# Chunked retention followed by a top-2 mixture of adapters: how the last, half-length chunk is routed, added up and stored

## The chip, the cores and the metric

The kernel runs on one core of a Trainium2 chip. The metric is the device time in microseconds (us) of one execution; the time before is 184.84 us, the median of three runs (184.58 to 186.25).

## What is computed

The reference has two parts. The first is retention: causal attention without a softmax, in which the score of query token i and key token j of a head is weighted with a power of that head's decay. There are 8 batches, 8 heads, 576 tokens and a head size of 64. The second is a mixture of eight low-rank adapters that works on each of the 4608 token rows of 512 numbers, with two experts per token, and adds its result to the row.

```python
# retention, per batch and head
scores = (q @ k.T) / sqrt(64)
D[i, j] = gamma[h] ** (i - j) if i >= j else 0.0
x = (scores * D) @ v                      # heads side by side: x is 4608 x 512
# mixture of adapters, per token row of x
logits = x @ w_gate                       # 8 experts
w = softmax of the two largest logits
delta = sum over those two experts e of  w[e] * ((x @ A[e]) @ B[e])   # A[e]: 512x16, B[e]: 16x512
out = x + delta
```

## The kernel before

**Tiling.** The 576 tokens of a batch are cut into four chunks of 128 tokens and one last chunk of 64. A unit of work in a full chunk is two batches, and each batch is one token tile g of 128 rows. In the last chunk a unit is four batches, because 64 tokens of two batches are put on the 128 partitions of one tile: rows 0 to 63 belong to one batch and rows 64 to 127 to the next. There are 18 units. The last chunk is units 16 and 17, called h and n in the code (lines 748 to 786), and each of them has two token tiles, g = 0 and g = 1.

**Stages.** Helpers named by a letter put one stage of a unit into the queues.

- stage_S, stage_Q and stage_R compute the retention output xT of a unit, with the feature on the partitions.
- stage_B(t) transposes xT back with TensorE and so starts the sum for the output in PSUM: tile po, one bank for each half cc of the head pairs, and in each bank the two token tiles g = 0, 1 side by side.
- stage_Z(t, gs) multiplies xT by the router and by all A at once into the PSUM tile pz; VectorE then takes the largest logits (MAX8, tile m) and the bias ns.
- stage_V computes the two routing weights with a sigmoid on ScalarE (tile sg). stage_W makes the mask cm and the weighted low-rank values zc on VectorE. It calls stage_V itself if that has not been done.
- stage_X transposes zc with TensorE (pzt) and ScalarE copies the result to zT.
- stage_Y multiplies zT by B, adding to po, copies po to the SBUF tile osb and stores osb to memory.

**Order.** Each engine works through its own queue in the order of the program: mm, vec and act (lines 80 to 87) chain every instruction to the one before it on its engine, and the profile shows their line numbers (81 for TensorE, 84 for VectorE, 87 for ScalarE). The order of the stages at the end is written out by hand in lines 748 to 786. PSUM has eight banks, which `bank` and `done` (lines 102 to 110) hand out in a ring, so that the bank that has been free longest is used next.

**The end of the kernel.** The routing of unit n is put in between: the product for g = 0 (stage_Z and stage_V), then stage_Y of unit h, then the product for g = 1, and stage_W for both afterwards. Then follow stage_B(n), two stage_X and two stage_Y. With `spread=True` stage_Y lets VectorE copy the half cc = 1 and ScalarE the half cc = 0.

**The stores.** In a full chunk each token tile is one transfer of 128 rows of 2 KB (line 606). In the last chunk each token tile is two transfers of 64 rows, one for each batch (line 611). They are put into the queue of SyncE, except that in the last unit the second of the two goes into the queue of ScalarE:

```python
            for x in range(2):
                n0 = S * (HALF * g + 2 * qd + x) + C * c
                q_ = nc.scalar if last and x == 1 else nc.sync
                q_.dma_start(out=out[n0 : n0 + L, :], in_=of[rows(x), g, :])
```

Of the kernel before, what the change touches and what calls it, by code (L numbers as in the profile page):

```python
# [18 lines left out]
def kernel(  # L19
# [63 lines left out]
    def vec(fn, **kw):  # L83
        chain("dve", getattr(nc.vector, fn)(**kw))  # L84

    def act(fn, **kw):
        chain("act", getattr(nc.scalar, fn)(**kw))  # L87
# [14 lines left out]
    def bank(shape, name, dtype=FP32):  # L102

        n = free.pop(0)
        x = pp.tile(shape, dtype, tag=f"bank{n}", name=name)
        held[id(x)] = n, x
        return x

    def done(*tiles):
        free.extend(held.pop(id(x))[0] for x in tiles)  # L110
# [141 lines left out]
    def rows(g):  # L252
        return slice(64 * g, 64 * g + 64)
# [215 lines left out]
            s["xT"].append(xt)  # L469
        done(*px)  # L470

    def stage_B(t):

        s = st[t]
        po = [bank([128, 2, HP, Dh], f"po{cc}") for cc in range(2)]
        for g in range(2):
            for dt in range(HP):
                for cc in range(2):
                    mm(
                        po[cc][:, g, dt, :],  # L480
                        lhsT=s["xT"][g][rows(cc), dt, :],
                        rhs=id64[rows(cc), :],
                        is_transpose=True,
                        start=(g == 0 and dt == 0),
                        stop=False,
                        skip_group_check=True,
                    )
        s["po"] = po

    BOTH = (0, 1)  # L490

    def stage_X(ts, gs=BOTH):
        todo = [(t, g) for t in ts for g in gs]
        n = len(todo)
        pzt = bank([128, n, 128], "pzt", FP16)
        for y, (t, g) in enumerate(todo):
            mm(
                pzt[:, y, :], lhsT=st[t]["zc"][g], rhs=ident16,
                is_transpose=True, start=True, stop=True,
            )  # L500
        zt = mo.tile([128, n, 128], FP16, tag=f"zT{n}", name="zT", bufs=2)
        act("copy", out=zt, in_=pzt)
        done(pzt)
        for y, (t, g) in enumerate(todo):
            st[t].setdefault("zT", {})[g] = zt[:, y, :]
# [32 lines left out]
    def stage_V(t, gs=BOTH):  # L538
        s = st[t]
        n = len(gs)  # L540
        lg, m8, ns, pz = s[("route", gs)]
        sg = mo.tile([128, n, E], FP32, tag=f"sg{n}", name="sg")
        for y in range(n):
            act(
                "activation",
                out=sg[:, y, :], in_=lg[:, y, :], func=AFT.Sigmoid,
                bias=ns[:, y : y + 1], scale=2.0,
            )
        s[("route", gs)] += (sg,)
# [23 lines left out]
            s.setdefault("zc", {})[g] = zc[:, y, :]  # L573
        done(pz)

    def stage_Y(t, gs=BOTH, spread=False, last=False):
        c, qd, sl = units[t]
        s = st[t]
        po = s["po"]
        if gs[0] == 0:  # L580
            s["osb"] = outp.tile([128, 2, HP, 2, Dh], FP32, tag="osb", name="osb")
        osb = s["osb"]
        bv = Bcat.rearrange("p (a o d) -> p a o d", a=HP, o=2)
        for cc in range(2):
            for g in gs:
                mm(
                    po[cc][:, g, :, :],
                    lhsT=s["zT"][g],
                    rhs=bv[:, :, cc ^ g, :],
                    start=False,  # L590
                    stop=True,
                    skip_group_check=True,
                )
        for cc in range(2):
            for g in gs:
                if spread and cc == 1:
                    vec("tensor_copy", out=osb[:, g, :, cc ^ g, :], in_=po[cc][:, g])
                else:
                    act("copy", out=osb[:, g, :, cc ^ g, :], in_=po[cc][:, g])
        if gs[-1] == 1:  # L600
            done(*po)
        of = osb.rearrange("p g a o d -> p g (a o d)")
        for g in gs:
            if c < NFULL:
                n0 = S * (QUAD * qd + 2 * sl + g) + C * c
                nc.sync.dma_start(out=out[n0 : n0 + C, :], in_=of[:, g, :])
                continue
            for x in range(2):
                n0 = S * (HALF * g + 2 * qd + x) + C * c
                q_ = nc.scalar if last and x == 1 else nc.sync  # L610
                q_.dma_start(out=out[n0 : n0 + L, :], in_=of[rows(x), g, :])  # L611

    issue(0)
    issue(1)
# [37 lines left out]
    for t in range(NU):  # L652
        if units[t][2] == 0:
            issue(quads.index(units[t][:2]) + 2, (0, 1, 2) if t <= LATE else (0,))
        if t == 0:
            spin(10)
            first_T()
            scale_k(0)
            fill_pick(3)
            gp.dma_start(  # L660
                out=AW[0][:, :, ER : ER + E], in_=moe_w_gate.rearrange("(t p) e -> p t e", p=128)
            )
            for ho in range(2):
                act("copy", out=asc[1][rows(ho)], in_=asc[0][rows(1 - ho)])
            act(
                "copy", out=gdec.rearrange("p a b d -> p a (b d)"),
                in_=gde.unsqueeze(2).broadcast_to((128, HP, 2 * Dh)),
            )
            stage_S(0)
            stage_U(0)  # L670
            stage_Q(0)
            stage_R(0)
            place_A()
            for ho in range(2):
                gp.tensor_copy(out=AW[1][rows(ho)], in_=AW[0][rows(1 - ho)])
            gp.dma_start(out=Bcat, in_=moe_B.rearrange("e r d -> (e r) d"))
            stage_T(1, ("qT",))
            stage_T(1, ("kT",), shared=True)
            scale_k(1)
            stage_Z(0)  # L680
            stage_S(1)
            stage_W(0)
            stage_U(1)
            stage_Q(1)
            stage_R(1)
            stage_T(2, ("qT",))
            stage_B(0)
            stage_X([0])
            stage_Z(1)
            stage_V(1)  # L690
            stage_Y(0, spread=True)
            stage_T(2, ("kT",), shared=True)
            stage_T(3)
            scale_k(2)
            scale_k(3)
            stage_S(2)
            stage_W(1)
            stage_S(3)
            for u in (2, 3):
                stage_U(u)  # L700
                stage_Q(u)
                stage_R(u)
            late_T(4)
            for ho in range(2):
                gp.tensor_tensor(
                    out=maskh[ho], in0=trih.unsqueeze(1).broadcast_to((128, HP, L)),
                    in1=heads(1, ho, L), op=ALU.mult,
                )
            continue
        if t < 4 or units[t][2] or not is_full(t):  # L710
            continue

        before, near = [u for u in (t - 4, t - 3) if u > 0], (t - 2, t - 1)
        here = (t, t + 1)
        for u in here:
            for b, nm in enumerate(("qT", "kT")):
                stage_S(u, (b,))
                if t > LATE:
                    stage_T(u + 2, (nm,))
            if t > LATE:  # L720
                scale_k(u + 2)
        for u in before:
            stage_B(u)
        stage_X(before)
        stage_Z(near[0])
        stage_V(near[0])
        for u in before:
            stage_Y(u)
        stage_Z(near[1])
        stage_V(near[1])  # L730
        if t > LATE:
            issue(t // 2 + 2, (1,))
        if units[t][0] > 0:
            for u in here:
                stage_Q(u)
        for u in near:
            stage_W(u)
        for u in here:
            if t > LATE and u == here[1]:
                issue(t // 2 + 2, (2,))  # L740
            stage_U(u)
            if units[t][0] == 0:
                stage_Q(u)
            stage_R(u)
        if t <= LATE:
            late_T(t + 2)
# [6 lines left out]
    stage_X([h - 4, h - 3])  # L753
    stage_Z(h - 2)
    stage_V(h - 2)
    stage_Y(h - 4, spread=True)
    stage_Y(h - 3, spread=True)
    stage_W(h - 2)
    stage_R(h)
    stage_S(n)  # L760
# [10 lines left out]
    stage_W(h)  # L771
    stage_R(n)
    stage_B(h)
    stage_Y(h - 1, spread=True)
    stage_X([h])
    stage_Z(n, (0,))
    stage_V(n, (0,))
    stage_Y(h, spread=True)
    stage_Z(n, (1,))
    for g in range(2):  # L780
        stage_W(n, (g,))
    stage_B(n)
    for g in range(2):
        stage_X([n], (g,))
    for g in range(2):
        stage_Y(n, (g,), spread=True, last=True)
# [1 line left out]
_INS = ['q', 'k', 'v', 'moe_w_gate', 'moe_A', 'moe_B']  # L788
_OUTS = [((4608, 512), 'float32')]
# [25 lines left out]
```

## Time and profile before

| | before |
|---|---|
| time, median of three runs | 184.84 us |
| span of the profiled execution | 183.6 us |
| TensorE busy | 174.5 us (95%) |
| VectorE busy | 115.4 us (63%) |
| ScalarE busy | 66.8 us (36%) |
| GpSimd busy | 58.2 us (32%) |
| memory traffic | 209 GB/s over the span |
| last computing instruction | starts at 179.27 us, takes 0.37 us |
| last two stores issued | 179.67 us |

The span is the time from the first to the last event of the profiled execution. The share of busy time tells which engine carries the kernel as a whole; the change is in the last 10 us, and there it is the order of waits that counts. In a timeline line the first number is the start in us from the beginning of the span, the second the duration in us; then follow engine, line, operation, output and inputs, and in square brackets how long the engine stood idle before it, and what it was waiting for. SPq and ACTq are the queues of SyncE and ScalarE, in which the transfers are issued.

### The profile page before, as it was taken

How to read it: one execution, taken by the hardware profiler on the slowest of the kernel's cores; microseconds unless marked ns; L12 is line 12 of the kernel's file. 1: busy time of each engine (PE TensorE's matmuls, PEld its weight loads, DVE VectorE, ACT ScalarE, POOL GpSimd, SP SyncE). 2: the span in 40 equal slices, each digit the busy share in tenths (PEclk: the TensorE clock that was granted, in tenths of full speed). 3: DMA queues.
4: the chain of work that ended last, by engine and by line, in shares of the span. 5: the costliest groups of instructions: out<-in, count | busy, mean ns of one | idle time of the engine just before them, and what ended most of it. 6: DMA issues, size and time to landing. Idle time of an engine off the chain costs nothing. (4 is left out here: it accounts for less than half of the span.)

```text
span 183.6 us, 8103 instructions
## 1 busy us (share of the span) xinstructions
PE 174.5 (95%) x3606; PEld 163.2 (89%) x3606; DVE 115.4 (63%) x294; ACT 66.8 (36%) x179; POOL 58.2 (32%) x69
## 2 busy tenths in 40 slices
PE   7898999999999999999999999999999999999970
PEld 2698989989999999989999999999999999999850
DVE  3785956969566926764468626781679248385660
ACT  3602054061406150475602751175307550132540
POOL 8877016062029202676023802262040005000000
PEclk9999999999999999999999999999999999999997
DMA  6999979899898998897699899997880060033175
GB/s 143 277 257 253 282 223 263 248 279 260 224 272 235 248 323 231 241 290 240 175 335 288 238 280 283 287 222 137 287 177 4 0 225 10 4 115 122 74 245 144
DMA packets 53283, 38.74 MB, mean 211 GB/s; under 512 B 26992, under 2 KB 48640, under 8 KB 53248
## 3 DMA queue, kind: packets, MB, share of 16 engines
q1 hardware_dynamic: 50688, 37.23, 71.8%
q10 hardware_dynamic: 2384, 0.85, 1.8%
q8 instruction: 28, 0.46, 1.0%
q0 software_dynamic: 176, 0.15, 0.5%
q14 instruction: 7, 0.06, 0.1%
HBM read 28.91 MB, written 9.44 MB: 209 GB/s over the span
## 5 line engine op out<-in xcount | busy, mean ns | idle before, releaser
L84 DVE TENSOR_TENSOR rt<-ps,mask 128x512 f32<-128x512 f32 x64 | 40.4, 684 | 9.6 <-PE ps L81 9.0
L264 POOL TENSOR_TENSOR k<-k,pack 128x512 f32<-128x512 f32 x32 | 32.6, 1044 | 26.9 <-PE pkT L81 19.5
L81 PE MATMUL pz<-AW,xT 128*128 128x136 f32 x288 | 37.2, 282 | 0.0
L423 POOL TENSOR_TENSOR P<-pn,gdec 128x512 f32<-128x512 f32 x12 | 15.3, 1278 | 68.2 <-DVE pn L84 64.0
L81 PE MATMUL ps<-qT,kT 64*128 64x128 f32 x512 | 34.8, 279 | 0.3 <-issue 0.3
L81 PEld LDWEIGHTS pz<-AW,xT 128*128 128x128 f32 x288 | 34.7, 190 | 0.2
L81 PEld LDWEIGHTS ps<-qT,kT 64*128 64x128 f32 x512 | 31.3, 188 | 1.7 <-issue 1.0
L81 PE MATMUL px<-rt,v 128*64 128x128 f32 x512 | 30.7, 273 | 0.0
L87 ACT COPY qT<-pqT 128x512 f32<-128x512 f32 (+1 forms) x33 | 16.8, 568 | 31.2 <-PE pqT L81 31.1
L81 PEld LDWEIGHTS px<-rt,v 128*64 128x64 f32 x512 | 27.7, 137 | 0.0
L84 DVE TENSOR_TENSOR xT<-px,asc 128x512 f32<-128x512 f32 x36 | 24.4, 688 | 4.0 <-PE px L81 2.6
L87 ACT COPY kT<-pkT 128x512 f32<-128x512 f32 x29 | 16.0, 600 | 27.7 <-PE pkT L81 17.8
L84 DVE COPY lg<-pz 128x16 f32<-128x16 f32 x17 | 3.0, 174 | 32.6 <-PE pz L81 32.6
L81 PE MATMUL pu<-v,k 128*64 128x64 f32 x512 | 18.1, 224 | 0.0
L87 ACT COPY osb<-po 128x256 f32<-128x256 f32 x60 | 17.5, 387 | 1.4 <-PE po L81 0.8
L81 PEld LDWEIGHTS pu<-v,k 128*64 128x64 f32 x512 | 16.6, 138 | 1.4 <-issue 1.0
L87 ACT ACTIVATE sg<-lg,ns 128x8 f32<-128x8 f32 x34 | 8.4, 293 | 25.2 <-DVE ns L84 24.8
L81 PE MATMUL pkT<-id,k 64*128 64x64 f32 x288 | 13.1, 225 | 1.5 <-DMA k<-in_k_dram 1.4
L81 PE MATMUL px<-qT,P 64*64 64x128 f32 (+1 forms) x512 | 14.3, 259 | 0.0
L81 PEld LDWEIGHTS pkT<-id,k 64*128 64x128 f32 x288 | 11.4, 139 | 2.8 <-issue 0.9
L84 DVE TENSOR_TENSOR pn<-pu,P 128x512 f32<-128x512 f32 x12 | 8.3, 692 | 8.3 <-PE pu L81 8.3
L81 PEld LDWEIGHTS px<-qT,P 64*64 64x64 f32 x512 | 12.6, 133 | 0.9
(54 smaller groups left out, 149.4 us busy)
## 6 DMA issues: line engine op xcount, KB each, us to landing
out_dram<-osb SPq DMA_DIRECT2D x32, 256.0 KB, 3.5
v<-in_v_dram SPq DMA_DIRECT2D x4, 512.0 KB, 7.1
q<-in_q_dram SPq DMA_DIRECT2D x3, 512.0 KB, 5.3
k<-in_k_dram SPq DMA_DIRECT2D x3, 512.0 KB, 7.3
out_dram<-osb SPq DMA_DIRECT2D x6, 128.0 KB, 2.3
q<-in_q_dram SPq DMA_DIRECT2D x2, 256.0 KB, 4.1
k<-in_k_dram ACTq DMA_DIRECT2D x2, 256.0 KB, 4.7
Arow<-in_moe_A_dram SPq DMA_DIRECT2D x1, 256.0 KB, 6.6
```

The costliest lines, as they stand in the source:

```text
L81: chain("pe", nc.tensor.matmul(*args, **kw))
L84: chain("dve", getattr(nc.vector, fn)(**kw))
L87: chain("act", getattr(nc.scalar, fn)(**kw))
L264: gp.tensor_tensor(out=kk[:, b], in0=kk[:, b], in1=gv[:, 0].unsqueeze(2).broadcast_to((128, H, Dh)), op=ALU.mult,)
L423: nc.gpsimd.tensor_tensor(out=Pt, in0=pn, in1=gdec, op=ALU.mult)
```

## The change

Three things are changed, all of them for the last chunk.

1. The stores of a token tile of the last chunk become one transfer from all 128 partitions. The destination is addressed as two batches of 64 rows of 512 numbers. All of them are issued from SyncE.
2. The two products for the routing of unit n stand one after the other, each followed at once by its sigmoid and its weighting, and stage_Y of unit h comes after both. The first transpose of stage_X(n) comes before stage_B(n), the second after it.
3. With `split=True` stage_B gives each token tile g of unit n PSUM banks of its own (pn, four banks), so that the matmuls for g = 1 don't share a bank with copies that read g = 0.

The aim is shorter waits at the end of the kernel and fewer, fuller transfers. `spread=True` becomes `copies=("act", "dve")`, which makes the same copies on the same engines; the third choice, a copy by GpSimd, is not used by any call. The core of the diff:

```diff
-    def stage_B(t):
+    def stage_B(t, split=False):
         s = st[t]
-        po = [bank([128, 2, HP, Dh], f"po{cc}") for cc in range(2)]
+        if split:
+            s["banks"] = {(cc, g): bank([128, HP, Dh], f"pn{cc}") for g in range(2) for cc in range(2)}
+            s["po"] = s["banks"]
+        else:
+            s["banks"] = {cc: bank([128, 2, HP, Dh], f"po{cc}") for cc in range(2)}
+            s["po"] = {(cc, g): s["banks"][cc][:, g] for g in range(2) for cc in range(2)}
+        po = s["po"]
...
-                        po[cc][:, g, dt, :],
+                        po[(cc, g)][:, dt, :],
...
-                        start=(g == 0 and dt == 0),
+                        start=((split or g == 0) and dt == 0),
...
         for g in gs:
             if c < NFULL:
                 n0 = S * (QUAD * qd + 2 * sl + g) + C * c
                 nc.sync.dma_start(out=out[n0 : n0 + C, :], in_=of[:, g, :])
                 continue
-            for x in range(2):
-                n0 = S * (HALF * g + 2 * qd + x) + C * c
-                q_ = nc.scalar if last and x == 1 else nc.sync
-                q_.dma_start(out=out[n0 : n0 + L, :], in_=of[rows(x), g, :])
+            b0 = HALF * g + 2 * qd
+            nc.sync.dma_start(
+                out=out.rearrange("(b s) d -> b s d", s=S)[b0 : b0 + 2, C * c : C * c + L, :],
+                in_=of[:, g, :],
+            )
...
-    stage_Y(h - 1, spread=True)
+    stage_Y(h - 1, copies=("act", "dve"))
     stage_X([h])
-    stage_Z(n, (0,))
-    stage_V(n, (0,))
-    stage_Y(h, spread=True)
-    stage_Z(n, (1,))
     for g in range(2):
+        stage_Z(n, (g,))
+        stage_V(n, (g,))
         stage_W(n, (g,))
-    stage_B(n)
+    stage_Y(h, copies=("act", "dve"))
+    stage_X([n], (0,))
+    stage_B(n, split=True)
+    stage_X([n], (1,))
     for g in range(2):
-        stage_X([n], (g,))
-    for g in range(2):
-        stage_Y(n, (g,), spread=True, last=True)
+        stage_Y(n, (g,), copies=("act", "dve"))
```

More of the change, by code (lines that the diff above doesn't have):

```diff
@@ L487, in stage_B @@
                     )
-        s["po"] = po
     BOTH = (0, 1)
@@ L574, in stage_W, with stage_Y @@
         done(pz)
-    def stage_Y(t, gs=BOTH, spread=False, last=False):
+    def stage_Y(t, gs=BOTH, copies=("act", "act")):
         c, qd, sl = units[t]
@@ L586, in stage_Y @@
                 mm(
-                    po[cc][:, g, :, :],
+                    po[(cc, g)],
                     lhsT=s["zT"][g],
@@ L595, in stage_Y @@
             for g in gs:
-                if spread and cc == 1:
-                    vec("tensor_copy", out=osb[:, g, :, cc ^ g, :], in_=po[cc][:, g])
+                o, i = osb[:, g, :, cc ^ g, :], po[(cc, g)]
+                if copies[cc] == "act":
+                    act("copy", out=o, in_=i)
+                elif copies[cc] == "dve":
+                    vec("tensor_copy", out=o, in_=i)
                 else:
-                    act("copy", out=osb[:, g, :, cc ^ g, :], in_=po[cc][:, g])
+                    chain("pool", gp.tensor_copy(out=o, in_=i))
         if gs[-1] == 1:
-            done(*po)
+            done(*s["banks"].values())
         of = osb.rearrange("p g a o d -> p g (a o d)")
@@ L690 @@
             stage_V(1)
-            stage_Y(0, spread=True)
+            stage_Y(0, copies=("act", "dve"))
             stage_T(2, ("kT",), shared=True)
@@ L755 @@
     stage_V(h - 2)
-    stage_Y(h - 4, spread=True)
-    stage_Y(h - 3, spread=True)
+    stage_Y(h - 4, copies=("act", "dve"))
+    stage_Y(h - 3, copies=("act", "dve"))
     stage_W(h - 2)
```

## The prediction

> **What bounds the kernel now.** I read the row of busy shares first (TensorE 95% over the span), then the slices: in the last two TensorE reads 7 and 0 and the transfers 7 and 5, so the tail is another stage with other limits, and the change touches it alone. The chain of waits, followed back from the last instruction, ends like this (start, duration, what):
>
> ```profile
> 178.18 0.43 DVE osb L84
> 178.61 0.02 issue
> 178.63 0.02 ACTq L611
> 178.65 0.04 issue
> 178.69 0.54 ACTq L611
> 179.23 0.04 issue
> 179.27 0.37 ACT osb L87
> ```
>
> ScalarE's last copy waits behind its own 0.54 us of issuing a store. The timeline of the tail shows a second wait there:
>
> ```profile
> 175.34 0.76 DVE L84 COPY osb<-po 128x256 f32<-128x256 f32 x2
> 176.27 0.17 DVE L84 MAX8 m<-pz 128x8 f32<-128x8 f32 x1 [0.17 <-PE pz L81]
> 177.30 0.29 DVE L84 TENSOR_TENSOR zc<-pz,cm 128x128 f16<-128x128 f32 x1
> 178.11 0.37 ACT L87 COPY osb<-po 128x256 f32<-128x256 f32 x1
> 178.53 0.39 PE L81 MATMUL po<-Bcat,zT 128*128 128x256 f16 x2 [0.40 <-ACT osb L87]
> 179.27 0.37 ACT L87 COPY osb<-po 128x256 f32<-128x256 f32 x1 [0.78 <-PE po L81]
> 179.67 0.50 ACTq L611 DMA_DIRECT2D out_dram<-osb  x1
> ```
>
> The matmuls for g = 1 wait 0.40 us until the copies of g = 0 have left the shared bank. Arithmetic ends at 179.64 us and the last two stores are issued at 179.67. By the answers on single issues these land 2.5 us (SyncE) and 2.8 us (ScalarE) later, at 182.5, and the span ends 1.1 us after that, at 183.6. So the tail is: last copy, issue, landing, 1.1 us of closing. The time outside the profile is 184.84 - 183.6 = 1.24 us more.
>
> The stores themselves (DMA groups of the page; KB each, us from issue to landing):
>
> ```profile
> out_dram<-osb SPq DMA_DIRECT2D x32, 256.0 KB, 3.5
> out_dram<-osb SPq DMA_DIRECT2D x6, 128.0 KB, 2.3
> out_dram<-osb ACTq DMA_DIRECT2D x2, 128.0 KB, 2.7
> ```
>
> And the rate while stores stream (windows; the last two columns are the share of the 16 DMA engines and GB/s):
>
> ```profile
> 174.40:174.80 0.40, 0.40 (x6) 0.40 (x5) 0.17 (x1) 0.16 (x1) 0.00 (x0) 1.00 1.05 410
> 175.60:176.00 0.40, 0.40 (x6) 0.40 (x4) 0.40 (x2) 0.40 (x3) 0.00 (x0) 1.00 1.06 405
> 178.40:178.80 0.40, 0.27 (x2) 0.10 (x1) 0.20 (x1) 0.09 (x1) 0.00 (x0) 1.00 0.99 231
> 179.20:179.60 0.40, 0.00 (x0) 0.00 (x0) 0.18 (x1) 0.33 (x1) 0.00 (x0) 1.00 1.02 220
> ```
>
> With all 16 engines busy, stores of 128 rows move 405 to 410 GB/s (first two lines), stores of 64 rows 220 to 231 (last two). That speaks for full-height stores. It also gives the price used below: 408/16 = 25.5 GB/s for one engine, so **one row of 2048 bytes costs one engine 80 ns**; with the share of 1.05 divided out it is 84 ns. I take 82.
>
> **What the Trainium skill says.**
> 1. "DMA: Bandwidth & Descriptors", section "Why a DMA increments its semaphore by 16 and not by 1", tells how many of the 16 engines a transfer runs on: the slowest dimension of size above 1 is taken of each of the two access patterns, and the number is the largest one up to 16 that divides both; from SyncE and ScalarE the lowest-numbered engines are used. The trace agrees where it can: every transfer in it has 64 or 128 as its slowest dimension, and stores fill all 16 engines. It holds no transfer with a small outer dimension.
> 2. The same page, "Rules for kernel authors", says that two transfers of disjoint partition halves gain nothing over one of 128 partitions. The trace is more definite: 231 against 410 GB/s.
> 3. "PSUM — Partial Sum Buffer", "PSUM bank collisions raise a hardware error", wants engines kept apart by bank and quadrant. The 0.40 us wait above is such a dependency between different columns of one bank.
>
> **The change part by part.**
>
> *Order of unit n.* The second product for the routing no longer stands behind the four matmuls of stage_Y(h): in the chain these took 0.44 us (174.87 to 175.31). It would end at 175.81 in place of 176.25. On VectorE the queue becomes MAX8, ns, cm, zc for g = 0 and the same for g = 1, with the two copies of unit h (0.76 us) behind all of it. First sg ends at 175.64 as now; cm and zc take 0.14 + 0.29 and end by 176.1; then MAX8 0.17, ns 0.16, the sigmoid 0.27, cm 0.14 and zc 0.29 with about 0.2 us of hand-overs: second zc ends at 177.35, against 177.60 now. **Gain 0.25 us.** The price: the copies of unit h move from 175.34 to 177.4 on VectorE and behind the second sigmoid (176.9) on ScalarE. SyncE waits for them: the first store of unit h, issued at 175.93 now, comes at 177.85, the second at about 178.3. Behind ScalarE's two copies also waits the first zT (177.6), and behind that stage_Y(n, 0) at 177.9. This is 0.15 us later than now.
>
> *Own banks.* The second pair of matmuls loses its 0.40 us wait and starts once the second zT is there, at 178.2 in place of 178.53. Ring of banks, counted by hand: four new banks come from the output of h - 1, a pzt and a pz read long before, so no new wait; cost 0.
>
> *No store issue on ScalarE.* 0.54 us leave its queue between the last two copies. ScalarE's two copies of unit n run at 178.2 to 179.0, VectorE's (behind those of h until 178.2) to 179.15. So arithmetic ends near 179.15, **0.5 us earlier**, and the last store is issued at about 179.3.
>
> *The stores.* Eight transfers of 64 rows become four of 128. The issue costs 0.33 to 0.55 us each on SyncE, so all four are in the queue by 179.8. The source is 128 partitions, but the destination is written as 2 batches of 64 rows: the stride from batch to batch (576 rows) is not 64 rows, so these two cannot be one dimension, and its slowest dimension is 2. By the skill's rule the transfer runs on 2 engines, since 2 is the largest number that divides 128 and 2. Each then carries 64 rows, 64 x 82 ns = 5.25 us, where 16 engines carry 8 rows each in 0.65 us. All four use the same two engines one after the other: 256 rows x 82 ns = 21.0 us. The fixed part of a landing, from the 256 KB store issued alone at 172.8 (2.1 us), is 2.1 - 0.65 = 1.45. Start of the first, plus fixed part, plus rows: 177.85 + 1.45 + 21.0 = 200.3. Closing 1.1: span 201.4. Outside the profile 1.24: 202.6. I say **203**, for the small gaps between transfers. With 80 ns and a first issue at 177.5 it is 201.8, with 86 ns and 178.3 it is 204.1; two engines alone could run at the skill's 27 GiB/s each ("Specifications" of that page; by my estimate 71 ns a row), which gives 199.8; not seen in this trace, where 80 ns is the least. That the gains before the stores are hidden under 20 us of draining follows: what ends last is the queue of two engines, and only the first issue counts for it, which has become 1.9 us later.
>
> **The rivals.**
>
> *All 16 engines are used after all* (the pattern is rewritten before it reaches the chip, or the split follows the source's 128 partitions). For it: the trace has no transfer on fewer. Then the four stores take 0.65 us each from 177.85 + 1.45 on, ending at 181.9, bound by that or by 179.3 + 2.1 = 181.4; closing 1.1, outside 1.24: **184.2 us**, 0.3% faster, within 1%. The 0.5 us won in arithmetic is mostly given back because the stores of h start late. A gain over 1% would need arithmetic to end 1.9 us earlier, and no wait in the tail is that long.
>
> *Two engines for a transfer, but other ones for each.* Then only the last counts: 179.3 + 1.45 + 5.25 + 1.1 + 1.24 = **188.3 us**, 1.9% slower. Against it: the rule names the lowest-numbered ones.
>
> *An engine becomes the bound*, the copies of h colliding with the routing of n: at worst all 0.76 us of VectorE's copies go on the path, on 16 engines 185.0 us, within 1%. I count it into the first rival.
>
> **How the numbers follow.** Two engines, the same ones: 0.85, at 203 us. 16 engines: 0.11, at 184.2 us, and of these 0.02 for faster by over 1%. Different pairs: 0.04, at 188.3 us. The range takes in the bounds of the first case, 199.8 to 204.1, and on each side some 3 us for a row's price on two lone engines, which no row of the trace shows: 197 to 207. That holds nearly all of the 0.85 and leaves out the rest, so about 8 in 10. Faster 0.02, same 0.09, slower 0.89.
>
> **What would show it.** Right: TensorE, VectorE and ScalarE all done by about 179.2, then some 20 us in which only transfers run, at a DMA share near 2/16 = 0.12 and near 50 GB/s; the four stores of the last chunk with landings that grow by about 5 us less the gap between issues, from 7 to some 21 us; the wait of the po matmul on the copies gone; first store of h after 177.5. Wrong: a tail at a share of 0.5 or more, landings of 2 to 4 us and a span near 183, which means 16 engines; landings of some 7 us each, which means different pairs; a share of 0.12 with far fewer GB/s than 50, which means that the price of a row was off.

## The result and the profile after

The changed kernel takes 204.09 us (median of four runs, 203.59 to 205.25), against 184.71 us of the kernel before in the same series. The ratio is 1.1045, with a 95% interval of 1.096 to 1.1131: 10.4% slower. The span of the profiled execution is 201.9 us in place of 183.6.

The arithmetic is not later. This profile ran about 1 us ahead of the one before up to the tail, so I count from a common mark, VectorE's first copy of unit h - 1 (173.81 us before, 172.84 after). The lines of the timeline that answer to those shown of before:

```profile
172.84 0.76 DVE L84 COPY osb<-po 128x256 f32<-128x256 f32 x2
...
175.17 0.16 DVE L84 MAX8 m<-pz 128x8 f32<-128x8 f32 x1
...
176.18 0.29 DVE L84 TENSOR_TENSOR zc<-pz,cm 128x128 f16<-128x128 f32 x1
...
176.64 0.76 DVE L84 COPY osb<-po 128x256 f32<-128x256 f32 x2 [0.17 <-issue]
...
176.65 0.86 PE L81 MATMUL pn<-Bcat,zT 128*128 128x256 f16 x4
...
177.01 0.79 ACT L87 COPY osb<-pn 128x256 f32<-128x256 f32 x2
...
177.13 9.98 SPq L619 DMA_DIRECT2D out_dram<-osb  x4
177.31 0.74 DVE L84 COPY osb<-pn 128x256 f32<-128x256 f32 x2
```

The last copy ends at 178.05, 5.21 us after the mark; before it was 179.64 - 173.81 = 5.83. The arithmetic won 0.62 us. No matmul of the last output waits for a copy any more. But the issue of four stores fills SyncE's queue for 9.98 us, and the span goes on for 23.8 us after the last copy. What fills it is told by the windows (the last two columns are the share of the 16 DMA engines and GB/s):

```profile
178.20:178.40 0.20, 0.00 (x0) 0.00 (x0) 0.00 (x0) 0.00 (x0) 0.00 (x0) 1.00 0.03 10
178.40:179.00 0.60, 0.00 (x0) 0.00 (x0) 0.00 (x0) 0.00 (x0) 0.00 (x0) 0.64 0.16 24
179.00:182.00 3.00, 0.00 (x0) 0.00 (x0) 0.00 (x0) 0.00 (x0) 0.00 (x0) 0.50 0.12 31
182.00:187.00 5.00, 0.00 (x0) 0.00 (x0) 0.00 (x0) 0.00 (x0) 0.00 (x0) 0.50 0.13 51
187.00:192.00 5.00, 0.00 (x0) 0.00 (x0) 0.00 (x0) 0.00 (x0) 0.00 (x0) 0.50 0.13 51
192.00:197.00 5.00, 0.00 (x0) 0.00 (x0) 0.00 (x0) 0.00 (x0) 0.00 (x0) 0.50 0.13 51
...
200.20:200.40 0.20, 0.00 (x0) 0.00 (x0) 0.00 (x0) 0.00 (x0) 0.00 (x0) 0.50 0.11 41
200.40:201.90 1.50, 0.00 (x0) 0.00 (x0) 0.00 (x0) 0.00 (x0) 0.00 (x0) 0.50 0.00 0
```

For 22 us (178.4 to 200.4) no engine computes, and the share of the DMA engines stays near 0.13, which is two of 16 (2/16 = 0.125). From 182 us on they move 51 GB/s, which is 25.5 for each of the two. The packets of this stretch also show where each store ends:

```profile
DMA packets 520, 1.05 MB, mean 44 GB/s; under 512 B 8, under 2 KB 8, under 8 KB 520
```

512 of them are the rows of 2 KB, 128 for each store. The other eight are small, and they come in pairs, at 185.0, 190.1, 195.2 and 200.4 us, each time behind the last of 128 rows. So the four stores end one after the other, 5.1 us apart, as they must if all of them share the same two engines. The waits of SyncE's queue tell the length of the drain in one line; line 820 is where the program closes:

```profile
SPq L820 <- DMA out_dram<-osb: 13.5, 1, 13.5
```

The chain that ended last doesn't show this. It ends with VectorE's last copies and closing, with no transfer in it; someone who reads only the chain would look for the loss in the arithmetic:

```profile
176.98 0.74 DVE osb L84 x2
177.72 0.33 DVEq L820
```

And the DMA group of the page is not suspicious either: it puts the four slow stores with 32 fast ones, and its median is lower than before (2.6 against 3.5 us).

```profile
out_dram<-osb SPq DMA_DIRECT2D x36, 256.0 KB, 2.6
```

### The profile page after: what moved, and what is told of

Its sections match the earlier page's. It is cut to its first block, busy times and chain, and to the rows that moved or that the text cites. A ratio compares the mean times of both kernels' runs of the same rounds, so it can differ in the third digit from the quotient of the medians.

```text
span 201.9 us, 8097 instructions
## 1 busy us (share of the span) xinstructions
PE 174.1 (86%) x3606; PEld 162.6 (81%) x3606; DVE 115.1 (57%) x294; ACT 66.7 (33%) x179; POOL 58.2 (29%) x69
## 5 line engine op out<-in xcount | busy, mean ns | idle before, releaser
L81 PE MATMUL ps<-qT,kT 64*128 64x128 f32 x512 | 34.1, 278 | 0.1
L81 PEld LDWEIGHTS ps<-qT,kT 64*128 64x128 f32 x512 | 30.7, 188 | 1.2 <-issue 0.7
L87 ACT COPY osb<-po 128x256 f32<-128x256 f32 x58 | 16.7, 388 | 0.6 <-ACT osb L87 0.6
L87 ACT ACTIVATE sg<-lg,ns 128x8 f32<-128x8 f32 x34 | 8.4, 293 | 25.2 <-DVE ns L84 24.8
```

The source lines that it names most:

```text
L81: chain("pe", nc.tensor.matmul(*args, **kw))
```

## The experiments

The theory is the prediction's: the outermost size of the destination, 2, puts each new store on the same two engines. The rivals are that the new order or the banks cost the time, that a destination of two dimensions is slow whatever its sizes, and that each transfer uses another pair of engines. The kernel before took 185.2 to 186.2 us in these later series, so ratios to it are compared, with 95% intervals.

**New order and banks, old stores.**

```diff
-            b0 = HALF * g + 2 * qd
-            nc.sync.dma_start(
-                out=out.rearrange("(b s) d -> b s d", s=S)[b0 : b0 + 2, C * c : C * c + L, :],
-                in_=of[:, g, :],
-            )
+            for x in range(2):
+                n0 = S * (HALF * g + 2 * qd + x) + C * c
+                q_ = nc.scalar if t == NU - 1 and x == 1 else nc.sync
+                q_.dma_start(out=out[n0 : n0 + L, :], in_=of[rows(x), g, :])
```

> New order and own banks kept, the last chunk stored as before in eight transfers of 64 rows. Theory (two engines carry each new store): the 20 us of draining are gone, 184.5 to 186.5 us; a little above 184.7 is likely, since the first store of unit h is now issued some 1.2 us later against the arithmetic, six issues of 0.55 us stand in SyncE's queue after it, and 64-row stores moved only 220 to 231 GB/s. Rival (the reorder or the new banks cost the time): it stays above 195 us.

Measured: 1.0088 (1.0048 to 1.0128). With the old stores the 10% are gone; what is left is 0.9% of loss, which belongs to the order or the banks. A later run tells which.

**Other outermost sizes.** The same four stores of 256 KB, with another shape of the destination: first 4 batches of 32 rows, then, in a second kernel, 8 batches of 16 rows. The rows of the last chunk change places in the output, so these two kernels serve for their times alone.

```diff
-            b0 = HALF * g + 2 * qd
+            i0 = C * c + 32 * qd
...
-                out=out.rearrange("(b s) d -> b s d", s=S)[b0 : b0 + 2, C * c : C * c + L, :],
+                out=out.rearrange("(b s) d -> b s d", s=S)[HALF * g : HALF * g + HALF, i0 : i0 + 32, :],
```

```diff
-            b0 = HALF * g + 2 * qd
+            i0 = C * c + 16 * (2 * qd + g)
...
-                out=out.rearrange("(b s) d -> b s d", s=S)[b0 : b0 + 2, C * c : C * c + L, :],
+                out=out.rearrange("(b s) d -> b s d", s=S)[:, i0 : i0 + 16, :],
```

> The changed kernel, but each store of the last chunk goes to 4 batches of 32 rows in place of 2 of 64 (the rows of the last chunk are permuted among themselves; same bytes, same four transfers). Theory (the engine count is the largest number that divides 128 and the outermost size, always the same lowest engines): 4 engines, 128 rows of 80 ns each = 10.2 us in place of 20.5, so 193.9 us, DMA share in the drain 0.25 and about 102 GB/s. Rival (a destination of two dimensions is slow as such, or SyncE's long issues set the pace): about 204 us as before. Rival (another set of engines for each transfer): only the last store counts, about 186 us.

Measured: 1.0613 (1.055 to 1.0676). A window in the middle of the drain and SyncE's closing wait:

```profile
188.00:192.00 4.00, 0.00 (x0) 0.00 (x0) 0.00 (x0) 0.00 (x0) 0.00 (x0) 0.50 0.26 102
```

```profile
SPq L820 <- DMA out_dram<-osb: 10.0, 1, 10.0
```

> As the run with 4 batches, but 8 batches of 16 rows. Theory: 8 engines, 64 rows of 80 ns = 5.1 us, 15.4 us less than the changed kernel: 188.7 us, DMA share in the drain 0.5 and about 200 GB/s. Rival of a slow two-dimensional destination: about 204 us.

Measured: 1.0304 (1.0232 to 1.0376). A late window of the drain:

```profile
186.00:187.00 1.00, 0.00 (x0) 0.00 (x0) 0.00 (x0) 0.00 (x0) 0.00 (x0) 0.50 0.51 197
```

The share of the engines is 0.13, 0.26 and 0.51 for outermost sizes of 2, 4 and 8, and the rate 51, 102 and 197 GB/s: the count of engines is the outermost size, and each carries about the same, 25 GB/s. The small packets agree: the four stores have 8, 16 and 32 of them, which is 2, 4 and 8 for each store. Two rivals fall with it. A two-dimensional destination that is slow as such would not care for the sizes. Other engines for each transfer would have let several of them run at once, at a multiple of these rates. From the first issue to the end of the span it is 24.8, 15.1 and 9.8 us (201.9 - 177.13, 195.0 - 179.89, 189.1 - 179.34); the steps, 9.7 and 5.3 us, are close to the 10.2 and 5.1 expected. The measured times came out some 2 us above what was written down. In the two profiled executions most of that lies ahead of the tail: the common mark is at 175.58 and 175.06 us, against 172.84. Why these ran later up to there is not known.

**The same kernel with 16 engines.**

```diff
+            if t < 2:
+                continue
...
-            b0 = HALF * g + 2 * qd
-            nc.sync.dma_start(
-                out=out.rearrange("(b s) d -> b s d", s=S)[b0 : b0 + 2, C * c : C * c + L, :],
-                in_=of[:, g, :],
-            )
+            n0 = S * (2 * qd + g)
+            nc.sync.dma_start(out=out[n0 : n0 + C, :], in_=of[:, g, :])
```

> The changed kernel, but each store of the last chunk goes to 128 consecutive rows, so that 128 is the outermost size on both sides; these are rows of the first chunk, whose own four stores (units 0 and 1) are left out, and the rows of the last chunk are not written. Theory: 16 engines, about 400 GB/s in the drain, 183.5 to 184.5 us: this is the changed kernel as the prediction's first rival had it (184.2). Rival (order or banks cost time): above 186 us.

Measured: 0.9967 (0.9936 to 0.9998). The drain:

```profile
178.40:180.00 1.60, 0.00 (x0) 0.00 (x0) 0.00 (x0) 0.00 (x0) 0.00 (x0) 1.00 1.06 406
180.00:181.00 1.00, 0.00 (x0) 0.00 (x0) 0.00 (x0) 0.00 (x0) 0.00 (x0) 0.87 0.76 291
```

One transfer for a tile is not what costs: with 128 as the outermost size on both sides it moves 406 GB/s. This run leaves out 1 MB of stores early in the kernel, so its 0.3% is no clean value for the rest.

**New stores alone.** The kernel before with the changed `dma_start` and nothing else.

> The kernel before with the new stores alone; order and banks as before. Theory (the drain of two engines starts with the first store of unit h and nothing else counts): the first store is issued about 2 us earlier than in the changed kernel, so 202 us, faster than the changed kernel although its arithmetic ends later. Rival (the loss comes from the new order together with the stores): near 184.7 us. Rival (the last store sets the end): above 204 us.

Measured: 1.0982 (1.0918 to 1.1046). The store alone brings the loss, so the last rival, order or banks, falls too as the cause of the 10%. The theory also says that the drain starts with the first store of unit h. That store is now issued 2.1 us after the mark, in place of 4.3:

```profile
174.52 0.76 DVE L84 COPY osb<-po 128x256 f32<-128x256 f32 x2
...
176.63 9.96 SPq L609 DMA_DIRECT2D out_dram<-osb  x4
```

The ratio is lower than that of the changed kernel (1.1045), but the two intervals overlap, so the times alone don't show the 2 us. The two profiles do: from the mark to the end of the span it is 26.8 us (201.3 - 174.52) here and 29.1 us (201.9 - 172.84) in the changed kernel, although the last copy here ends later, 5.6 us after the mark in place of 5.2.

**Banks alone, and larger transfers.** The first of three kernels has the order and the stores as before, with `split=True`. The second adds to this that the last unit is stored in two transfers of 64 partitions with both tiles in each. The third stores both units so, with the new order; its edit is:

```diff
...
+            if g == 1:
+                ob = out.rearrange("(g b s) d -> b s g d", g=2, s=S)
+                for x in range(2):
+                    q_ = nc.scalar if t == NU - 1 and x == 1 else nc.sync
+                    q_.dma_start(out=ob[2 * qd + x, C * c : C * c + L], in_=of[rows(x)])
```

> Order and stores as before, own banks for the two tiles of unit n alone. Theory: the 0.40 us wait of the second pair of po matmuls goes, but ScalarE still issues a store between its last two copies; 0.1 to 0.4 us faster than before, 184.3 to 184.6 us, within 0.2%. Rival (the wait is hidden by the issue on ScalarE): no change at all.

Measured: 1.0000 (0.9961 to 1.0038). No gain is seen, as the rival had it, though the interval doesn't exclude the gain of at most 0.2% that was expected. The wait is gone, and the profile shows the arithmetic 0.55 us earlier against the mark (5.28 us in place of 5.83), but the stores don't follow:

```profile
174.07 0.76 DVE L84 COPY osb<-po 128x256 f32<-128x256 f32 x2
...
176.19 3.89 SPq L621 DMA_DIRECT2D out_dram<-osb  x6
...
178.44 0.91 DVE L84 COPY osb<-pn 128x256 f32<-128x256 f32 x2 [0.59 <-PE pn L81]
178.94 1.40 ACTq L621 DMA_DIRECT2D out_dram<-osb  x2
```

ScalarE issues its two stores in 1.40 us, until 180.34. That is 6.27 us after the mark; before it was 180.17 - 173.81 = 6.36. ScalarE's last store is issued behind its first, so nearly all of the 0.55 us is lost again before the last issue ends. Compared with the first run above, which differs from this one only in the order, the order costs 0.9%.

> Order as before, own banks, and the last unit stored in two transfers of 64 partitions with both tiles in each (two rows of 2 KB from each partition; the outermost size stays 64, so 16 engines), one from SyncE and one from ScalarE after the last copy. Theory: last issue some 0.6 us earlier than before, a landing of about 0.3 us more: 184.1 to 184.6 us, a candidate that beats both. Rival (half-height data at 220 GB/s is the bound at the end): 184.7 us or more.

Measured: 1.0031 (1.0003 to 1.0059).

> New order and own banks, both units of the last chunk stored in two transfers of 64 partitions with both tiles in each (four transfers, 16 engines each). Theory: arithmetic ends 0.6 us earlier than before, but 1 MB leaves at half height at 220 GB/s from a first issue that is later: 184.3 to 185.5 us. Rival (issue time on SyncE was all that mattered): 183.8 us or less.

Measured: 1.0139 (1.0086 to 1.0192). Both expectations failed. The issues are not what costs: in the last of these runs SyncE's issues end 6.7 us after the mark (180.16 + 2.03 - 175.54), in the run with the new order and the old stores 8.1 us after it (177.73 + 3.77 - 173.44), and yet the span goes on to 11.6 us after the mark against 11.2. The loss lies in the drain. That it comes of waiting for both tiles before either is stored is likely, but no run tells it apart from the rate of half-height stores.

**One transfer on 16 engines, with the right rows.** If the partitions take the tokens of the two batches in turn, the destination can be walked token by token, and its outermost size is 64:

```diff
-                out=xt.rearrange("p a (y i) -> p a y i", y=2),
+                out=xt.rearrange("p a (i y) -> p a y i", y=2),
...
-                out=out.rearrange("(b s) d -> b s d", s=S)[b0 : b0 + 2, C * c : C * c + L, :],
+                out=out.rearrange("(b s) d -> s b d", s=S)[C * c : C * c + L, b0 : b0 + 2, :],
```

> The changed kernel with the tokens of the two batches interleaved on the partitions (xT of the last chunk is written with token outside and batch inside), so that one transfer of 128 partitions goes to a destination of 64 rows by 2 batches: the outermost sizes are 128 and 64. Theory (the loss is the outermost size of 2 and nothing else of the one-transfer store): 16 engines, a drain of about 3 us, 0.3% faster than before as the run with consecutive rows was, some 20 us faster than the changed kernel. Rival (any two-dimensional destination loses): above 188 us.

Measured: 1.0006 (0.9973 to 1.0039). The drain:

```profile
178.80:180.00 1.20, 0.00 (x0) 0.00 (x0) 0.00 (x0) 0.00 (x0) 0.00 (x0) 1.00 1.00 388
180.00:181.00 1.00, 0.00 (x0) 0.00 (x0) 0.00 (x0) 0.00 (x0) 0.00 (x0) 0.69 1.04 401
```

The destination still has two dimensions, and all 16 engines work; the small packets are 64 now, 16 for each store. Against the changed kernel only the order of the rows on the partitions differs, and the 10% are gone. The gain of 0.3% over the kernel before did not come; the interval just excludes it.

> As the interleaved run, with own banks, but unit n routed in the order of the kernel before, so that the stores of unit h are issued early. Theory: arithmetic ends 0.55 us earlier than before, the last store lands in 2.1 us in place of 2.5 to 2.8 and doesn't stand behind the stores of h: 0.9 to 1.2 us faster than before (0.5 to 0.65%), faster than the interleaved run with the new order. Rival (the new order is worth having once the stores are cheap): slower than that run.

Measured: 0.9929 (0.9899 to 0.9959). This version, with own banks, the order of before and interleaved stores, is faster than both kernels: by 0.7% than the one before.

> The kernel before with the interleaved one-transfer stores alone; its order and shared banks. Theory: ScalarE no longer issues a store between its last two copies (0.3 us) and the landing is shorter by 0.4 to 0.7 us, while the bank wait of 0.40 us stays: 0.6 to 0.9 us faster than before, between the kernel before and the run with own banks and the old order.

Measured: 0.9959 (0.993 to 0.9987). The interleaved store alone brings 0.4%. That the banks add something to it is likely but not shown, since the intervals overlap; that the new order takes 0.8% away (0.9929 against 1.0006) is shown, for the second time. The profiles tell where. These are SyncE's four issues with the new order and with the old one, both interleaved and with own banks:

```profile
177.21 2.63 SPq L619 DMA_DIRECT2D out_dram<-osb  x4
```

```profile
176.58 3.92 SPq L619 DMA_DIRECT2D out_dram<-osb  x4
```

With the marks at 172.92 and 174.46 the first issue is 4.3 and 2.1 us after the mark, and the last one ends 6.9 and 6.0 us after it. The time from the mark to the end of the span, in one profiled execution each, is longer with the new order whatever the store:

| stores of the last chunk | order before | new order |
|---|---|---|
| two halves, own banks | 9.7 us | 11.2 us |
| one transfer, outermost size 2 (order before: shared banks) | 26.8 us | 29.1 us |
| one transfer, interleaved, own banks | 8.9 us | 9.9 us |

## Why the prediction was right

The mechanism was the right one, two engines that carry all four stores one after the other, and the time forecast, 203, is 1.1 us below the measured one. That it came so close is partly luck, as the term for the time outside the profile shows below. By its own steps:

- *Two engines, the same two for all four stores.* Right, and shown: by the outermost sizes 2, 4 and 8, by the stores that end 5.1 us apart, and by the interleaved run. The Trainium skill's rule in "DMA: Bandwidth & Descriptors", section "Why a DMA increments its semaphore by 16 and not by 1", held in every run; the kernel before had no transfer that could have tested it. The runs have powers of two alone, so they don't tell "the largest number that divides both sizes" from "the smaller size, at most 16", and the trace doesn't number the engines, so that they are the lowest ones is not shown.
- *Price of a row.* 82 ns was taken. In the steady part it is 80 ns (2048 bytes at 25.5 GB/s), and 256 rows would have been 20.5 us. The drain took 22.0 (178.4 to 200.4), because its first 3.6 us ran at 24 and 31 GB/s: 107 KB where 51 GB/s would have moved 184, a loss of 77 KB or 1.5 us. This term, 21.0 us in the sum, was 1.0 us too small: the 82 in place of 80 covers a third of what the slow first rows cost. The 27 GiB/s for an engine that the Trainium skill gives ("DMA: Bandwidth & Descriptors", "Specifications") were not reached: 25.5 GB/s is 23.7 GiB/s.
- *Fixed parts.* 1.45 us for a landing and 1.1 for closing were taken, 2.55 in all. Measured are 1.3 from the first issue to the first row and 1.5 from the last row to the end of the span: 2.8.
- *Time outside the profile.* 1.24 us was taken, the median of three runs less the span of another execution. The profiled execution of the kernel before took 185.32 us itself, so outside its span lie 185.32 - 183.6 = 1.7 us; after the change it is 203.59 - 201.9 = 1.7. Rows, fixed parts and this term together were 1.7 us too small. The profiled execution of the changed kernel hides 0.7 of it, since it ran 1 us ahead up to the tail and issued the first store at 177.13 in place of 177.85, and the rounding from 202.6 up to 203 hides another 0.4.
- *First store of h later.* Forecast 4.04 us after the mark (177.85 - 173.81), measured 4.29 (177.13 - 172.84); before 2.12. That this first issue alone counts for the end is borne out by the run with the new stores alone.
- *Gains of the arithmetic.* Forecast 0.5 us, measured 0.62. The second zc came 0.15 us earlier against the mark in place of 0.25.
- *Bank wait.* It went, as said. In the run with the banks alone the earlier matmuls brought no gain in time that could be seen (1.0000, within 0.4%).
- *All stores in the queue by 179.8.* Wrong: SyncE stood in the issue of the third and fourth until 187.1. The landings that the prediction gave as a sign therefore grew less than it said: from issue to the end of the store it is 7.9 us for the first (177.1 to 185.0) and 18.2 for the fourth (182.2 to 200.4), not 21. The two engines had work all the time, so the wait of SyncE itself cost nothing that can be seen; whether the slow first rows, which fall in the issue of the third store (178.6 to 182.1), have to do with it is open.
- *Full height against half height.* "231 against 410 GB/s" picked the low windows of the half-height stores. A window of the same trace, a little later, has them at 333 GB/s:

```profile
180.40:180.80 0.40, 0.00 (x0) 0.00 (x0) 0.00 (x0) 0.00 (x0) 0.00 (x0) 1.00 0.91 333
```

So the contrast of nearly two to one is not a fixed one. The forecast doesn't rest on it.
- *The rival with 16 engines, 184.2 us.* That the gain is given back because the stores of h start late was right and too mild: with 16 engines and the right rows, new order and banks come to 1.0006, and with the old stores to 1.0088.

## What to carry to other kernels

Before two transfers are joined into one, write down the outermost size of both access patterns: if it is small, the joined transfer may be spread over that many DMA engines only, and here 256 KB on two of them took 5.1 us in place of about 0.65 (256 KB at 406 GB/s). The remedy is not to split the transfer again but to choose which row lies on which partition, so that a long dimension can be walked outermost. And when the order of work is changed near the end, look at when the earlier stores are issued as well as at when the last instruction ends: here 0.6 us of arithmetic were bought with stores 2 us later.

## What the runs showed that I had not expected

- An issue can hold its queue. In the changed kernel SyncE's third store took 3.5 us to issue and the fourth 4.9 us, while the drain went on; in the profile these times look like work of SyncE. Why they take so long was not tried.
- The drains on 2, 4 and 8 engines start slowly: 31 GB/s at a share of 0.12 (two engines, 179 to 182 us), then 51. With full-height stores on 16 engines no such stretch is seen (406 GB/s from 178.4 us on). What slows the first rows was not tried and stays open.
- Half-height stores are not always slow. With the new order and the old stores they moved 207 to 211 GB/s at a share of 0.89 to 0.94 from 179 to 181 us, and 334 at 1.05 in the next microsecond. The kernel before has both rates as well, 220 to 231 and 333 GB/s. What decides between them stays open.
